# A spectral layer before two mixtures of experts: the order of relu, maximum and inverse copies, and weights loaded a step sooner

## Chip, cores and metric

The kernel runs on one core of one Trainium2 chip. The metric is the device time of one execution in microseconds, as the median over runs. The profile is of one further execution of the same program, with the span from its first to its last instruction.

## The reference, cut to what matters

```python
def _attn_ref(x, w_r, w_i, b_r, b_i):            # x: 8 x 3072 x 256
    X = np.fft.rfft(x, axis=1)
    Yr = Xr @ w_r - Xi @ w_i + b_r
    Yi = Xr @ w_i + Xi @ w_r + b_i
    lam = 0.01
    Yr = np.sign(Yr) * np.maximum(np.abs(Yr) - lam, 0.0)
    Yi = np.sign(Yi) * np.maximum(np.abs(Yi) - lam, 0.0)
    return np.fft.irfft(Yr + 1j * Yi, n=3072, axis=1)

def _moe_ref(x, w_in, w_out):                    # w_in: 256 x 2048
    h = x @ w_in
    return (h - np.tanh(h)) @ w_out

def _moe2_ref(x, phi, w1, w2):                   # 32 slots, 8 experts
    logits = x @ phi                             # softmax over tokens gives the slots' inputs,
    ...                                          # each expert works on its slots,
    return (c @ slot_out).astype(np.float32)     # softmax over slots gives the outputs
```

The spectral part works on each of the 8 batches: a real Fourier transform over 3072 positions, a complex 256 x 256 product per frequency, a shrinkage towards zero by 0.01, and the inverse transform. The two mixtures follow over all 24576 tokens. w_in and w_out arrive as 64-bit floats.

## The kernel before, in words

The kernel has a spectral phase (`spectral_phase`), a token phase (`token_phase`, a written-out plan of matrix products per chunk of tokens) and an expert phase. Every engine runs its instructions in the order in which the program issues them, and one SP queue issues nearly all DMAs; the order is written out by hand.

Each transform is split in two. The spectral phase is one loop over steps `s` (lines 604 to 660): 8 batches of 12 steps, and 12 more in which the last batch is finished and the token phase starts beside it. In step `s` the loop issues work of several batches at once:

- `f2_pair` (295): the second forward transform of pair `s`. TensorE makes `pf` (301); ScalarE copies it to `xmf` (310) and rounds it to `xmh` (312); VectorE makes the sum of both parts `xms` (322) and the rest `xml` (325).
- `part` (392): ScalarE's relu `c` (395) for the pair that was mixed in the step before. It reads `t`, which `shrink` finished.
- `i2_half` (445): half of a piece of the second inverse transform of an earlier batch. TensorE makes `pi` (455) in one PSUM bank that all halves share; ScalarE copies it to `yt` (462). The next half can only be written when the copy has read the bank. `i2_at` lists the halves of each step: one half in most steps, two in steps 8 to 11 of a batch (counted in its 12 steps) from the second batch on, and two in each of steps 88 to 95 (three in 88) and 100 to 107.
- `split_sum` (331): ScalarE rounds `xms` (333), GpSimd takes the rest (334).
- `mix_part` (346): three groups of six products of the pair of the step before: `pa`, and two into `pmix` (344).
- `add_bias` (366): VectorE adds the bias to `pa`, into `t` (376). It reads `pa`'s only bank, which the next step's first group overwrites.
- `join` (399): VectorE's maximum of `t` and `-c` into `sw` (402), for the pair of the relu; the result of the shrinkage.
- `shrink` (383): VectorE adds `pmix` to `t` (386).
- `i1_four` (411), every fourth step: the first inverse transform of four pairs (`px`, 420), of which the last one's `sw` is made in the same step; copies to `vs` by ScalarE (409) and VectorE (407), stored in the next step.
- `f1_piece` (253), in steps 0, 2, 4 and 6 of a batch two of them: the first forward transform (`px`, 262) of the next batch, copied by ScalarE to `asb` (267), stored by `flush` in the next step (172). The `asb` tiles alternate between two buffers.
- Weights: `load_w` (480) loads 256 KB of w_out or w_in as pairs of 32-bit words into `raw`, which has one buffer. `due_w` sets the step: piece `j` at step `3j - 2`. Two steps later `narrow` (528) queues nine VectorE operations ("chores") that make 32-bit floats of it; `pump` issues one, three and one of them per step. `use_w` (489) and `fold_w` (510) use the piece three and four steps after that; pieces of w_out, up to step 49, need a transpose (505) and a small product (518) on TensorE.
- Loads a few steps ahead: `load_x` (183), `load_v2` (432), `load_a2` (283); stores of `yt` by `store_y` (470).

The order of the parts before the change:

```python
                part()
                pump(1)
                ...
                due = i2_at.get(s, ())
                for j in due[:(len(due) + 1) // 2]:
                    i2_half(*j)
                if s < T:
                    split_sum(b, i)
                pump(3)
                if m:
                    mix_part(*m, 0)
                    add_bias(*m)
                join()
```

Of the kernel before, what the change touches and what calls it, by code (L numbers as in the profile page):

```python
# [11 lines left out]
I32 = mybir.dt.int32  # L12
# [130 lines left out]
def spectral_phase(tc, nb, x, w_r, w_i, b_r, b_i, tb, yd, w_in, w_out, phi, ident, wo32, wh, wl, wp, ew):  # L143

    nc = tc.nc
    with ExitStack() as late, ExitStack() as mid, ExitStack() as ctx:
# [12 lines left out]
        dcp = ctx.enter_context(tc.tile_pool(name="fdc", bufs=1))  # L159
# [38 lines left out]
        def load_f2(g0, g1):  # L198
            nc.sync.dma_start(out=f2[:, 128 * g0:128 * g1], in_=tb["f2"][:, 128 * g0:128 * g1])
# [17 lines left out]
        def load_mix():  # L217
            for w in (w_r, w_i):
                t = thp.tile([128, 512], F32, tag="sw", name="wst", bufs=5)
                nc.sync.dma_start(  # L220
                    out=t.rearrange("p (h e) -> p h e", h=2), in_=w.rearrange("(h p) e -> p h e", p=128)
                )
                tables.append(t)
# [59 lines left out]
        def load_a2(b, i):  # L283

            if i % 2 == 0:
                t = a2p.tile([128, 4, D], F32, tag="a2", name="a2")
                src = ad[b].rearrange("(g k) (n d) -> (k n) g d", k=2, n=M2)[:, 2 * i:2 * i + 4, :]
                for g in ((slice(0, 2), slice(2, 4)) if (b, i) == (0, 0) else (slice(0, 4),)):
                    nc.sync.dma_start(out=t[:, g], in_=src[:, g])
                a2[b, i] = t[:, 0:2]  # L290
                a2[b, i + 1] = t[:, 2:4]
# [100 lines left out]
        def part():  # L392
            for b, i, t in below:
                c = thp.tile([128, 512], F32, tag="c", name="c", bufs=1)
                nc.scalar.activation(c, t, AF.Relu, bias=lam2, scale=-1.0)  # L395
                both.append((b, i, t, c))
            below.clear()

        def join():
            for b, i, t, c in both:  # L400
                v = sh[b, i] = thp.tile([128, 512], F32, tag="sw", name="sw", bufs=5)
                nc.vector.scalar_tensor_tensor(out=v, in0=c, scalar=-1.0, in1=t, op0=ALU.mult, op1=ALU.max)
            both.clear()
# [41 lines left out]
        def i2_half(b, j, u):  # L445

            t = v2[b, j]
            h, n = divmod(j, 4)
            i = 2 * n + u
            if i == 0:  # L450
                yt[b, h] = yp.tile([128, 6, 512], F32, tag=f"y{h}", name="yt")
            p = next(i2_homes).tile([128, 4, 128], F32, tag="i2", name="pi2")
            for a in range(4):
                n2 = 4 * i + a
                nc.tensor.matmul(  # L455
                    p[:, a, :], t[:, 4 * u + a, :], i2[:, 96 * n2:96 * n2 + 128], start=True, stop=True
                )
            y = yt[b, h]
            src = p[:, :, 0:96].rearrange("p a (c k r) -> p a c k r", k=4, r=4)
            n = 5 if b == nb - 1 else 6  # L460
            o = y[:, 0:n].rearrange("p c (a k r l) -> p a c k r l", k=4, a=4, l=8)[:, :, :, :, :, i]
            nc.scalar.activation(o, src[:, :, 0:n], AF.Copy)  # L462
            if n < 6:

                o = y[:, n:6].rearrange("p c n -> p (c n)").rearrange("p (m a r l) -> p a m r l", a=4, r=4, l=8)[:, :, :, :, i]
                nc.scalar.activation(o, p[:, :, 16 * n:96].rearrange("p a (m r) -> p a m r", r=4), AF.Copy)
            if u == 1:
                del v2[b, j]
# [10 lines left out]

        def load_w(j):  # L480
            src, r, q = pieces[j]
            raw = dcp.tile([128, 256, 2], I32, tag="raw", name="raw", bufs=1)
            nc.sync.dma_start(
                out=raw,
                in_=src[128 * r:128 * r + 128, 256 * q:256 * q + 256].bitcast(I32).rearrange("p (n t) -> p n t", t=2),
            )
            wraw[j] = raw
# [35 lines left out]
        def pump(n):  # L523
            for f, *args in chores[:n]:
                f(*args)
            del chores[:n]
# [31 lines left out]
        if True:  # L558
            load_f2(0, 2)
            for i in range(8):  # L560
                f1_piece(0, i, i % 2)
            load_mix()
            load_a2(0, 0)
            split_mix()
            load_a2(0, 2)
            load_f2(2, 8)
            load_w(0)
            load_x(1, 0)
            load_tables()
            load_f2(8, 16)  # L570
            load_late_tables()
            load_x(1, 1)
            load_f2(16, NG)
            load_x(1, 2)
            T = nb * NP

            pieces_at = {}
            for k in range(1, nb):
                for j, t in enumerate((2, 2, 3, 4, 4, 6, 6, 7) if k == 1 else (0, 0, 2, 2, 4, 4, 6, 6)):
                    pieces_at.setdefault(NP * (k - 1) + t, []).append((k, j))  # L580

            def piece(t):
                return pieces_at.get(t, [])

            i2_at, v2_at, y_steps = {}, {}, {}
            for k in range(nb):
                t = NP * k + NP
                if k < nb - 2:
                    steps = [t + 5 + j for j in range(3)] + [t + 8 + j // 2 for j in range(8)] + [t + 12 + j for j in range(5)]
                    gap = 1  # L590
                else:
                    steps = [t + 4 + j // 2 for j in range(16)]
                    gap = 1
                for j in range(8):
                    for u in range(2):
                        i2_at.setdefault(steps[2 * j + u], []).append((k, j, u))
                    v2_at.setdefault(max(t + 2, steps[2 * j] - 3), []).append((k, j))
                for h in range(2):
                    for u in range(3):
                        t1 = steps[8 * h + 7] + 1 + gap * u  # L600
                        y_steps.setdefault(t1 if k < nb - 1 else T + NP - 1, []).append((k, h, 2 * u))

            due_w = {max(3 * j - 2, 2 * j - 1): [j] for j in range(len(pieces))}
            for s in range(T + NP):
                b, i = divmod(s, NP)
                flush()
                if s < T:
                    f2_pair(b, i)
                part()
                pump(1)  # L610
                for j in due_w.get(s - 2, ()):
                    narrow(j)
                for j in piece(s + 4):
                    load_x(*j)
                m = divmod(s - 1, NP) if 1 <= s <= T else None
                for j in v2_at.get(s, ()):
                    load_v2(*j)
                due = i2_at.get(s, ())
                for j in due[:(len(due) + 1) // 2]:
                    i2_half(*j)  # L620
                if s < T:
                    split_sum(b, i)
                pump(3)
                if m:
                    mix_part(*m, 0)
                    add_bias(*m)
                join()
                if m:
                    mix_part(*m, 1)
                for j in due_w.get(s - 6, ()):  # L630
                    fold_w(j)
                for j in due_w.get(s - 5, ()):
                    use_w(j)
                for j in due[(len(due) + 1) // 2:]:
                    i2_half(*j)
                if m:
                    mix_part(*m, 2)
                    shrink(*m)
                pump(2 if s < 8 else 1)
                if s % 4 == 1 and 5 <= s <= T + 1:  # L640
                    i1_four(*divmod((s - 5) // 4, NP // 4))
                for k, j in enumerate(piece(s)):
                    f1_piece(*j, k)
                for j in y_steps.get(s, ()):
                    store_y(*j)
                if 4 <= s < 12:
                    load_i2(s - 4)

                for t in (s + 2, s + 4):
                    if 4 <= t < T and (t == NP) == (t == s + 2):  # L650
                        load_a2(*divmod(t, NP))
                for j in due_w.get(s, ()):
                    load_w(j)
                if s == T:
                    ctx.close()
                if s == T + 3:
                    mid.close()
                    more = late.enter_context(tc.tile_pool(name="fpe", bufs=1, space=PSUM, side="right"))
                    i2_homes = cycle((more, psl))
                yield  # L660
# [927 lines left out]
```

## Time and profile before

| | us |
|---|---|
| median of 3 runs | 2059.61 (2059.58 to 2060.22) |
| the profiled execution | 2055.87 |
| its span | 2054.1 |
| TensorE busy in it | 1956.1 (95%) |
| VectorE busy | 1698.1 (83%) |
| ScalarE busy | 1341.9 (65%) |

Times in the profile are microseconds from the start of the span. PE is TensorE's products, PEld its loads of weights, DVE VectorE, ACT ScalarE, POOL GpSimd, SPq the queue of SyncE that issues DMAs. L395 is line 395. An arrow in a name reads "out<-in". A row of waits has the engine that waited, what it waited for, the total, the times and the longest.

### The profile page before, as it was taken

The numbers are of one execution on the slowest core, as the hardware profiler recorded it, in microseconds if no ns is written. First come the engines' busy times: TensorE is split into PE (matmuls) and PEld (weight loads), VectorE is DVE, ScalarE is ACT, GpSimd is POOL, SyncE is SP. The second block draws the span as 40 slices with busy tenths as digits, with TensorE's granted clock in tenths as the row PEclk, the third lists the DMA queues.
The fourth block names the chain that finished last, engine by engine and source line by source line (L and its number), as shares of the span: only waits on it lengthen the run. The fifth ranks groups of instructions, "written<-read, shape, count | busy, mean of one in ns | idle before, by whom it ended". The sixth has DMA issues, their size and how long they took to land.

```text
span 2054.1 us, 53297 instructions
## 1 busy us (share of the span) xinstructions
PE 1956.1 (95%) x20542; PEld 1680.4 (82%) x20542; DVE 1698.1 (83%) x3389; ACT 1341.9 (65%) x2496; POOL 1180.3 (57%) x1022
## 2 busy tenths in 40 slices
PE   6899999999999999999999999999999999999875
PEld 3678888888888898888888888888888888898633
DVE  4777777777777899999999999999999999999745
ACT  3566767677666777666666676766666667676425
POOL 0111111221113888888888888888888888888300
PEclk9899999999999999999999999999999999999996
DMA  9789999999656677777777777777777777777899
GB/s 269 236 263 277 290 293 283 294 285 304 205 185 202 155 183 178 180 177 177 177 180 180 174 182 185 177 179 180 176 178 178 179 173 183 186 174 182 252 382 385
DMA packets 249788, 445.59 MB, mean 217 GB/s; under 512 B 35392, under 2 KB 143680, under 8 KB 249280
## 3 DMA queue, kind: packets, MB, share of 16 engines
q1 hardware_dynamic: 248496, 440.59, 79.4%
q8 instruction: 163, 2.67, 0.6%
q10 hardware_dynamic: 1040, 1.61, 0.2%
q14 instruction: 89, 0.73, 0.1%
HBM read 139.01 MB, written 105.91 MB: 119 GB/s over the span
## 4 chain that ended last, share of the span: by engine, by line
PE 79%; DMA 8%; ACT 7%; DVE 3%; SPq 1%; issue 1%; ACTq 0%; DVEq 0%
PE ph L819 45%; PE pl L935 8%; PE pd L1055 8%; PE pmix L344 4%; PE pi L455 4%; PE pf L301 3%; PE px L262 2%; PE px L420 2%; ACT yt L462 1%; DMA out_dram<-gq 1%; PE pa L344 1%; ACT xmf L310 1%; PE ph L789 1%; ACT xmh L312 1%; ACT c L395 1%
## 5 line engine op out<-in xcount | busy, mean ns | idle before, releaser
L872 POOL TENSOR_TENSOR g<-g,tanh 128x512 f32<-128x512 f32 x558 | 709.1, 1298 | 159.4 <-ACT tanh L860 159.3
L830 ACT ACTIVATE g<-ph 128x512 f32<-128x512 f32 x564 | 333.1, 591 | 228.7 <-PE ph L819 219.5
L884 DVE STREAM_TRANSPOSE gt<-g 128x512 f32<-128x512 f32 x752 | 479.0, 679 | 0.6 <-POOL wl L749 0.3
L819 PE MATMUL ph<-th,s 128*128 128x256 f32 x2256 | 455.8, 285 | 0.7 <-ACT g L830 0.7
L845 DVE TENSOR_TENSOR g<-ph,g 128x512 f32<-128x512 f32 x564 | 372.7, 680 | 68.8 <-ACT g L830 35.2
L860 ACT ACTIVATE tanh<-g 128x512 f32<-128x512 f32 x564 | 336.9, 621 | 102.5 <-DVE g L845 63.7
L819 PEld LDWEIGHTS ph<-th,s 128*128 128x128 f32 x2256 | 369.4, 190 | 20.2 <-issue 19.4
L334 POOL TENSOR_TENSOR xml<-xms,xmh 128x256 fp32r<-128x256 f32 x96 | 76.7, 799 | 511.8 <-ACT xmh L333 332.8
L819 PE MATMUL ph<-tl,s 128*128 128x256 f32 x1128 | 318.5, 282 | 0.0
L819 PE MATMUL ph<-yh,wl 128*128 128x256 f32 x1128 | 315.9, 280 | 0.0
L819 PE MATMUL ph<-yh,wh 128*128 128x256 f32 x1128 | 315.2, 279 | 0.0
L819 PE MATMUL ph<-y,wh 128*128 128x256 f32 x1128 | 315.1, 279 | 0.0
L819 PEld LDWEIGHTS ph<-tl,s 128*128 128x128 f32 x1128 | 214.9, 190 | 0.0
L819 PEld LDWEIGHTS ph<-yh,wh 128*128 128x128 f32 x1128 | 212.9, 189 | 0.1
L819 PEld LDWEIGHTS ph<-y,wh 128*128 128x128 f32 x1128 | 212.1, 188 | 0.0
L819 PEld LDWEIGHTS ph<-yh,wl 128*128 128x128 f32 x1128 | 212.0, 188 | 0.0
L935 PE MATMUL pl<-g,wp 128*32 128x256 f32 x3072 | 184.8, 381 | 0.0
L1055 PE MATMUL pd<-gq,et 128*32 128x256 f32 x3008 | 170.9, 379 | 0.0
L455 PE MATMUL pi<-i,v 96*128 96x128 f32 x1024 | 138.9, 280 | 16.9 <-ACT yt L462 15.6
L716 POOL TENSOR_TENSOR tl<-tr,th 128x512 fp32r<-128x512 f32 x94 | 121.8, 1297 | 56.9 <-ACT th L715 30.8
L1055 PEld LDWEIGHTS pd<-gq,et 128*32 128x32 f32 x3008 | 97.8, 110 | 64.5
L935 PEld LDWEIGHTS pl<-g,wp 128*32 128x32 f32 x3072 | 94.6, 110 | 64.4 <-issue 0.9
(209 smaller groups left out, 4146.5 us busy)
## 6 DMA issues: line engine op xcount, KB each, us to landing
gq<-gt SPq DMA_DIRECT2D x1504, 128.0 KB, 2.3
xt<-in_x SPq DMA_DIRECT2D x64, 448.0 KB, 7.9
vd<-vs SPq DMA_DIRECT2D x48, 512.0 KB, 4.7
v<-vd SPq DMA_DIRECT2D x64, 384.0 KB, 6.3
yd<-yt SPq DMA_DIRECT2D x48, 512.0 KB, 6.1
y<-yd SPq DMA_DIRECT2D x48, 512.0 KB, 3.5
a<-ad SPq DMA_DIRECT2D x47, 512.0 KB, 7.2
ad<-asb SPq DMA_DIRECT2D x114, 192.0 KB, 5.0
```

The lines of the kernel that those rows point to most:

```text
L334: nc.gpsimd.tensor_tensor(out=lo[:, 0], in0=sm, in1=hi[:, 0].bitcast(F32), op=ALU.subtract)
L344: nc.tensor.matmul(o, st[u], w[m], start=first and k == 0, stop=last and k == 2)
L455: nc.tensor.matmul(p[:, a, :], t[:, 4 * u + a, :], i2[:, 96 * n2:96 * n2 + 128], start=True, stop=True)
L716: nc.gpsimd.tensor_tensor(out=lo, in0=t, in1=hi.bitcast(F32), op=ALU.subtract)
L819: nc.tensor.matmul(o[:, 256 * j:256 * j + 256], a[u][:, 128 * j:128 * j + 128], y[v], start=new and j == 0 and k == 0, stop=n in (2, 3, 4) ...
L830: nc.scalar.activation(e[n], o.rearrange("p (j n) -> p j n", j=2), AF.Copy)
L845: nc.vector.tensor_tensor(out=h, in0=o, in1=h, op=ALU.add)
L860: nc.scalar.activation(t, g, AF.Tanh)
L872: eng.tensor_tensor(out=g, in0=g, in1=th.pop((c, w, n)), op=ALU.subtract)
L884: nc.vector.transpose(out=t[:, :, :, 2 * (p % 4) + u, :], in_=g[:, u, :].rearrange("p (q k i) -> p q k i", q=4, k=4))
L935: nc.tensor.matmul(lp[c][q:q + 32, 0:256], wp[:, 2 * p + f, :], half_of(c, gs[c, p + f // 2][:, f % 2], h), start=p == 0 and f < 2, stop=p ...
L1055: nc.tensor.matmul(o[32 * a:32 * a + 32, f], ex[c][:, k, :], g[a][:, k], start=k == 0, stop=k == 3)
```

## The change

In steps with two or more halves the relu (`part`) is issued behind the first of the two groups of halves and their copies, not ahead of them; in step 88 that group has two halves. The maximum (`join`) is issued ahead of the bias sum (`add_bias`) in every step. `raw` gets a second buffer, and `load_w` is called one step sooner.

```diff
         def load_w(j):
             src, r, q = pieces[j]
-            raw = dcp.tile([128, 256, 2], I32, tag="raw", name="raw", bufs=1)
+            raw = dcp.tile([128, 256, 2], I32, tag="raw", name="raw", bufs=2)
...
                 if s < T:
                     f2_pair(b, i)
-                part()
+                due = i2_at.get(s, ())
+                if len(due) < 2:
+                    part()
                 pump(1)
...
-                due = i2_at.get(s, ())
                 for j in due[:(len(due) + 1) // 2]:
                     i2_half(*j)
+                if len(due) > 1:
+                    part()
                 if s < T:
                     split_sum(b, i)
                 pump(3)
+                join()
                 if m:
                     mix_part(*m, 0)
                     add_bias(*m)
-                join()
-                if m:
                     mix_part(*m, 1)
...
-                for j in due_w.get(s, ()):
+                for j in due_w.get(s + 1, ()):
                     load_w(j)
```

## Rows read from the trace of the kernel before

**Rows 1.** The page: the chain that ended last, shares of the span by engine.
```profile
PE 79%; DMA 8%; ACT 7%; DVE 3%; SPq 1%; issue 1%; ACTq 0%; DVEq 0%
```

**Rows 2.** Window: busy PE, PEld, DVE, ACT, POOL, granted clock, DMA share, GB/s.
```profile
197.00:269.00 72.00, 70.31 (x725) 60.70 (x724) 53.91 (x108) 49.67 (x83) 9.53 (x12) 1.00 0.97 292
```

**Rows 3.** Waits from 40 to 690 us.
```profile
PEld pi L455 <- ACT yt L462: 22.2, 32, 2.1
PE pi L455 <- ACT yt L462: 15.6, 29, 1.9
ACT asb L267 <- DMA ad<-asb: 14.8, 3, 11.2
```

**Rows 4.** Chain (start, us): a mixing group, a half without wait.
```profile
593.12 0.71 PE pmix L344 x6
...
207.25 0.89 PE pi L455 x8
```

**Rows 5.** Timeline of step 91 (start, us, engine, line, operation).
```profile
577.89 1.06 PE L455 MATMUL pi<-i,v 96*128 96x128 f32 x8
578.09 0.60 ACT L310 ACTIVATE xmf<-pf 128x512 f32<-128x512 f32 x1 [0.70 <-PE pf L301]
579.31 0.71 ACT L395 ACTIVATE c<-t,lam 128x512 f32<-128x512 f32 x1
579.49 0.28 PE L344 MATMUL pmix<-wbh,xmh 128*128 128x256 f32 x1
579.93 0.86 ACT L462 ACTIVATE yt<-pi 128x384 f32<-128x384 f32 x1
580.05 0.28 DVE L536 TENSOR_SCALAR dl<-da 128x256 int32<-128x256 int32 x1
580.84 1.16 PE L455 MATMUL pi<-i,v 96*128 96x128 f32 x8 [0.47 <-ACT yt L462]
581.91 0.68 DVE L376 TENSOR_TENSOR t<-pa,bias 128x512 f32<-128x512 f32 x1
583.65 0.60 ACT L310 ACTIVATE xmf<-pf 128x512 f32<-128x512 f32 x1 [0.71 <-PE pf L301]
```

**Rows 6.** Chain: one transpose and one fold of a weight piece.
```profile
215.63 0.22 PE pt L505 x2
221.85 0.36 PE pw L518 x4
```

**Rows 7.** Timeline of step 68.
```profile
438.29 0.68 DVE L376 TENSOR_TENSOR t<-pa,bias 128x512 f32<-128x512 f32 x1
439.11 0.36 PE L344 MATMUL pa<-wah,xmh 128*128 128x256 f32 x1
441.73 1.16 PE L455 MATMUL pi<-i,v 96*128 96x128 f32 x8 [0.54 <-ACT yt L462]
```

**Rows 8.** Step 88: its second half, and the window around it.
```profile
557.42 0.80 PE L455 MATMUL pi<-i,v 96*128 96x128 f32 x2 [1.88 <-ACT yt L462]
...
557.00:559.00 2.00, 1.58 (x7) 1.58 (x8) 1.06 (x4) 0.37 (x1) 0.00 (x0) 0.59 1.05 396
```

**Rows 9.** Chain in step 37.
```profile
259.28 0.60 DVE t L376
259.88 0.61 DVE sw L402
```

**Rows 10.** SP's wait (200 to 560 us), landings of L172, VectorE's wait.
```profile
SPq L483 <- DVE dl L542: 46.5, 10, 11.4
...
DMA to landing us min/median/max: 2.9/5.1/7.8
...
DVE da L536 <- DMA raw<-in_moe_w_out: 6.3, 2, 6.0
```

**Rows 11.** Windows of two steps one after the other.
```profile
254.46:260.49 6.03, 5.79 (x72) 5.00 (x71) 4.12 (x9) 3.84 (x8) 0.74 (x1) 1.00 1.06 378
260.49:266.52 6.03, 5.99 (x72) 4.95 (x76) 4.96 (x8) 3.89 (x6) 0.71 (x1) 1.00 0.73 233
```

## The prediction, made before any run of the change

> **What bounds the kernel now.** I read the page's chain first, then the windows of the spectral phase, then its waits, then the chain and the timeline of single steps. The page's chain that ended last lies on TensorE for 79% of the span [rows 1], so a gain has to be TensorE time. The token phase leaves TensorE no gap that this change touches; all edits lie in the step loop of the spectral phase. There a batch of 12 steps takes about 72 us, with TensorE busy for 70 of them at the full granted clock and the DMA engines at a share of 0.97 [rows 2]. The table of waits of that phase names what TensorE stands for: the second inverse half waits for the copy L462 29 times on the products' side and 32 times on the weights' side; hardly anything waits for a DMA except ScalarE's copy of the first transform, 3 times [rows 3].
>
> Two halves stand in steps 20 to 23, 32 to 35, 44 to 47, 56 to 59, 68 to 71, 80 to 83 (six batches of four) and 88 to 95: 32 "double steps" that also have a relu, as many as there are waits. Behind such a wait the second half's products take 1.16 [rows 5] instead of 0.89 [rows 4], because they start cold. The timeline of step 91 gives the geometry [rows 5]. Counted from the start of ScalarE's xmf copy (578.09): relu at +1.22, copy of the first half at +1.84, second half at +2.75, next xmf at +5.56. TensorE would have been free at +2.11: its middle mixing group starts at +1.40 (579.49) and six such products take 0.71 [rows 4]. So 0.64 us per double step is TensorE standing for ScalarE.
>
> **Part 1, the copy ahead of the relu.** Without the relu in front the copy starts one ScalarE slot earlier. That slot is 579.93 - 579.31 = 0.62 us [rows 5]. The copy's own input is there: the first half's products begin at 577.89 and take 1.06, so they end at +0.86, before +1.22. The second half then starts at +2.13, where TensorE is free at +2.11: the gain is 0.62, and what is late next is TensorE itself. Bounds per step: 0 (something else holds it), and 0.89, if the cold start (1.16 against 0.89) goes too. I take 0.62, because a wait of 0.02 is left and the cold start may be left with it.
> Where weight pieces of w_out pass, TensorE has a transpose (0.22) or a fold (0.36) ahead of the second half, work that now fills the gap [rows 6]; up to step 47 each four double steps hold one of either. So:
> - steps 20 to 23, 32 to 35, 44 to 47: 3 x (0.62 + 0.62 + 0.40 + 0.26) = 5.7 us.
> - steps 56 to 59, 68 to 71, 80 to 83: 3 x 4 x 0.62 = 7.4 us. In the first of each four part 2 delays this step's first mixing group: in step 68 it starts 0.14 after the bias sum ends (438.97 and 439.11), so with the bias sum 0.60 later it loses about 0.5. Two groups of 0.71 follow, and the second half can start at about 441.05 where it started at 441.73 [rows 7]: 0.62 stands.
> - step 88 has three halves, two of them ahead of the relu; the second stood idle for 1.88 and the granted clock then fell to 0.59 of full speed in the mean of two us, so mostly to its 1.2 GHz level [rows 8]. I take 0.6 there and keep 1.4 as the upper bound, if the shorter wait leaves the clock at 2.4 GHz (0.41 of that window's 2 us back). Steps 89 to 95: 7 x 0.62 = 4.3.
> Together 18.0 us. The waits bear the size out from above: 15.6 us of idle products [rows 3] and 32 cold starts of 0.27 are 24.2 us lost in all, and the transposes, the folds and what is left of the cold starts stay.
>
> What the later relu holds up: the moved half brings its eight products and one copy, no DMA; on ScalarE the sum's split L333 keeps its place in time, as relu and copy only change places, and with it GpSimd's L334, which follows it. The maximum, and now the bias sum behind it, wait for the relu. The relu starts at +1.22 + 0.86 = +2.08 at the latest and ends at +2.79 [rows 5]; the maximum ends at about +3.4, the bias sum at +4.0 (0.60 each [rows 9]). Who waits for that is the next step's first mixing group, in step 91 at about 0.7 after the next xmf, so at 4.94 + 0.7 = +5.6: 1.6 us of cover (the next xmf comes at 5.56 - 0.62 = 4.94; of the middle group's +1.40 the first takes 0.71 [rows 4, 5]). With four weight chores ahead (580.05 to 581.91, 1.86 us [rows 5]) VectorE reaches the maximum only at about +3.8 and ends the bias sum at +5.1: 0.5 of cover, the thinnest. I cost the later relu at nothing; without that cover it costs up to 0.6 in 8 steps, 5 us.
>
> **Part 2, the maximum ahead of the bias sum.** In every fourth step the first inverse transform needs this step's maximum. In step 37 VectorE runs the bias sum for 0.60 and then the maximum for 0.61, and the chain goes on from there to the rest of that transform [rows 9]. With the order turned the maximum ends 0.60 earlier. The steps that look so are 13, 25, 37, 49, 61, 73 and 85, which all have four chores on VectorE: 7 x 0.60 = 4.2. Steps 5 and 9, in the start, show the same order in the timeline, one of them with half the wait: 0.3 + 0.6. The other transform steps have no chores, or are double steps and counted. Together 5.1, bounds 0 and 5.4 (nine times 0.60). The bias sum's delay is covered as above.
>
> **Part 3, weights sooner, two buffers.** The same DMAs in the same number; SP issues each (256 KB) a step earlier, ahead of the next step's stores and loads. What goes is SP standing for the single buffer: 46.5 us in ten waits, the longest 11.4 [rows 10], with the stores of the next step queued behind it. Nothing on TensorE waits for these now, so I take 0. Above, 6.0: VectorE's one long wait for a piece [rows 10], in the start. There the order of the DMAs in the queue is the same after the change, so I do not count on it. Below, a piece moved ahead of a store delays it by 256 KB at 290 GB/s [rows 2], 0.9 us; ScalarE waited only 3 times for such stores [rows 3], so -3 (3 x 0.9, rounded).
>
> **Sum.** 18.0 + 5.1 + 0 = 23.1 us. The profiled execution took 2055.87 us (span 2054.1), so it would take 2032.8. The median of the runs is 2059.61, 3.7 above the profiled one; taken from that, 2036.5 is the forecast. What a measurement of this kernel can tell from no change is about 0.2%, 4.1 us.
>
> **Rivals.**
> 1. DMA becomes the bound. For: a share of 0.97 over 72 us. 3.1 us less per batch makes it 1.01. If 1.00 were the ceiling, a batch could lose only 0.03 x 72 = 2.2; five batches give 11, the last, with less traffic, 5: 16 us, 2044 (2040 to 2050). Against: 1.06 at 378 GB/s for 6 us right beside 0.73 [rows 11], so the share has room and the queue has holes, some of them made by the SP waits that part 3 removes. Chance 0.15. The Trainium skill (DMA: Bandwidth & Descriptors, "Where 436 GB/s comes from") puts the engines' ceiling at 435 GB/s and HBM's part for a core at 358; by either, about 300 GB/s would not bind and this rival would fall. The trace agrees in so far as it has 378 in one window [rows 11].
> 2. VectorE becomes the bound in double steps: the relu comes late, maximum and bias sum behind it, and the next mixing group waits. At 0.3 per double step 10 us go, 2046; it decides where the bias sum ends after +5.5. For: 0.5 of cover with four chores. Against: VectorE is busy for 54 of 72 us [rows 2]. Chance 0.08.
> 3. Slower. The first transform's tiles alternate between two buffers; the store goes out one step after the copy and must land before the copy two steps on, some 6 us. Stores land in 2.9 to 7.8, median 5.1 [rows 10]. With fuller DMA and a weight piece ahead (0.9), the median reaches 6 and ScalarE, and with it xmf and TensorE, stands in each of three such steps a batch: 21 x 1.5 = 32 us against 23 won, 2068. It decides at a median landing of 6 us. Against: three such waits in all, 11.2 of their 14.8 us in one [rows 3], and SP's earlier issues. Chance 0.05. The Trainium skill (DMA: Bandwidth & Descriptors, "Queues, rings and completion order") has the rule behind this rival: each DMA engine takes the descriptors of a queue in ring order, so a piece issued ahead of the stores is moved ahead of them. By that rule alone, with all 31 moved pieces delaying the chain by 0.9, 28 us would be lost against 23 won; no row here shows a piece ahead of a store that was waited for.
> 4. The copy is not what the second half waits for in truth (a wait for two semaphores put down to one), and of part 2 half is hidden: 2.5 us, 2057. The rows against it: copy end and start of the second half agree within 0.05 us in step 91. Chance 0.06.
>
> **How the numbers follow.** The sum holds with 0.66, between 2031 (clock kept, some cold starts gone, a gain of 29) and 2044 (two thirds of it). Range of all: 2030 to 2051, which leaves out rivals 3 and 4 and the edges of the rest. Faster: 0.66 + 0.15 + 0.08 = 0.89; same 0.06; slower 0.05.
>
> **What would show it.** Right: the 32 waits of the second half for L462 are gone or under 0.1 us each; step 91 takes 4.9 to 5.0 instead of 5.56; step 37's maximum ends 0.6 earlier; SP no longer waits at L483; batches of about 69 us. Wrong: new waits of the mixing group for L376 in double steps (rival 2), of ScalarE's L267 for DMA (rival 3), or batches that stop at 70 us with a DMA share of 1.00 (rival 1).

## The result, and the profile after

| us | kernel before | changed kernel |
|---|---|---|
| median | 2059.6 (4 runs, 2056.57 to 2060.22) | 2040.73 (4 runs, 2038.83 to 2044.91) |
| the profiled execution | 2055.87 | 2041.15 |
| its span | 2054.1 | 2039.4 |

The ratio of the times is 0.9914, with a 95% interval of 0.9896 to 0.9932: 18.9 us faster between the medians. The forecast was 2036.5 (2030 to 2051), 4.2 us below the result. Between the two profiled executions only 14.7 us of span have gone; this text follows those, and comes back to the medians at the end.

The chain that ended last, by engine, on the page of the changed kernel:

```profile
PE 84%; DMA 8%; ACT 3%; DVE 2%; SPq 1%; issue 1%; ACTq 0%; DVEq 0%
```

ScalarE's part fell from 7% to 3% and TensorE's rose from 79% to 84% [rows 1]. Of the waits of the second half for its copy, 32 and 29 [rows 3], three are left on either side, in steps 88, 90 and 92. Three rows of the waits of that stretch in the changed kernel (engine, line, what it waited for: total, times, longest):

```profile
PEld pi L455 <- ACT yt L462: 5.0, 3, 2.8
...
PE pi L455 <- ACT yt L462: 4.4, 3, 2.6
...
ACT yt L462 <- DMA yd<-yt: 2.6, 1, 2.6
```

The third row is new: ScalarE's copy stood for a store. It comes back below. Step 91 in the timeline of the changed kernel, which answers to [rows 5]:

```profile
559.70 0.60 ACT L310 ACTIVATE xmf<-pf 128x512 f32<-128x512 f32 x1 [0.71 <-PE pf L301]
...
560.92 0.90 ACT L462 ACTIVATE yt<-pi 128x384 f32<-128x384 f32 x1
...
561.59 0.69 ACT L395 ACTIVATE c<-t,lam 128x512 f32<-128x512 f32 x1
...
561.87 1.16 PE L455 MATMUL pi<-i,v 96*128 96x128 f32 x8
...
562.79 0.36 PE L344 MATMUL pmix<-wch,xmh 128*128 128x256 f32 x1
...
564.67 0.60 ACT L310 ACTIVATE xmf<-pf 128x512 f32<-128x512 f32 x1 [0.68 <-PE pf L301]
```

The copy starts at +1.22 (it was +1.84), the second half at +2.17 with no wait shown (forecast +2.13), the next xmf at +4.97 (it was +5.56, forecast 4.94). The second half's eight products still read 1.16, but the next product starts 0.92 behind them. In the kernel before it started 0.91 behind as well (580.84 and 581.75 in step 91). So 1.16 against 0.89, which the prediction read as a cold start, is none: a timeline row runs to the modelled end of its products, the chain's piece only to the next start.

Two batches, in windows of the changed kernel (the columns of [rows 2]):

```profile
197.00:267.00 70.00, 69.95 (x730) 61.23 (x730) 54.06 (x109) 50.05 (x84) 10.96 (x12) 1.00 1.02 303
315.28:383.57 68.29, 67.84 (x710) 59.11 (x709) 53.60 (x107) 50.01 (x80) 12.91 (x15) 1.00 1.00 302
```

TensorE is busy for all but 0.05 of the first 70 us, with the DMA share at 1.02 where it was 0.97: what bounds this batch is TensorE itself. VectorE in step 37 of the changed kernel, the maximum now ahead of the bias sum [rows 9]:

```profile
256.24 0.68 DVE L402 SCALAR_TENSOR_TENSOR sw<-c,t 128x512 f32<-128x512 f32 x1
256.84 0.68 DVE L376 TENSOR_TENSOR t<-pa,bias 128x512 f32<-128x512 f32 x1
```

The maximum starts at +3.84 from the step's xmf (252.40), where it was +4.51 (259.88 and 255.37); in this step VectorE is no longer in the chain. Landings of the stores of L172 from 200 to 560 us [rows 10]:

```profile
DMA to landing us min/median/max: 3.0/5.5/7.9
```

SP's waits at L483 for VectorE's L542, 46.5 us in ten, are gone from that stretch.

**Where the 14.7 us came from.** The starts of xmf (L310) cut the loop into steps. Worked out from them, before minus after, in us:

| steps | measured | forecast |
|---|---|---|
| 20 to 23, 32 to 35, 44 to 47 | 2.01 + 1.99 + 1.99 = 6.0 | 5.7 |
| 56 to 59, 68 to 71, 80 to 83 | 2.37 + 2.34 + 2.34 = 7.05 | 7.4 |
| 88 | 9.41 - 7.25 = 2.15 | 0.6 |
| 89, 90, 91, 94 | 0.57 + 0.62 + 0.59 + 0.57 = 2.35 | 4 x 0.62 |
| 92 and 93 | -3.05 + 0.08 = -3.0 | 2 x 0.62 |
| 13, 25, 37, 49, 61, 73, 85 | 0.60 + 0.60 + 0.59 + 0.61 + 0.80 + 0.59 + 0.47 = 4.3 | 4.2 |
| 0 to 11 (the start) | 74.17 - 74.00 = 0.2 | 0.9 |
| 12 | 6.04 - 7.87 = -1.8 | 0 |
| the other steps from 14 to 87 | -0.2 | 0 |
| up to the xmf of step 95 | 16.95 | 22.5 (23.1 with step 95's 0.62) |

The first xmf starts 0.37 later and what follows step 95 takes 1.9 longer: 14.7. That tail lies between 1450.5 and 1454.8 in all twelve profiles of this study, before at 1451.6 and after at 1453.5, and follows no part of the change.

### The profile page after: what moved, and what is told of

Read it like the earlier page. It is cut to its first block, busy times and chain, and to the rows that moved or that the text cites. A ratio compares the mean times of both kernels' runs of the same rounds, so it can differ in the third digit from the quotient of the medians.

```text
span 2039.4 us, 53251 instructions
## 1 busy us (share of the span) xinstructions
PE 1952.4 (96%) x20542; PEld 1683.5 (83%) x20542; DVE 1699.8 (83%) x3389; ACT 1342.5 (66%) x2496; POOL 1185.1 (58%) x1022
## 3 DMA queue, kind: packets, MB, share of 16 engines
q8 instruction: 163, 2.67, 0.6%
## 4 chain that ended last, share of the span: by engine, by line
PE 84%; DMA 8%; ACT 3%; DVE 2%; SPq 1%; issue 1%; ACTq 0%; DVEq 0%
PE ph L821 45%; PE pl L937 8%; PE pd L1057 8%; PE pmix L344 5%; PE pi L455 5%; PE pf L301 4%; PE pa L344 3%; PE px L262 2%; PE px L420 2%; DMA xt<-in_x 2%; DMA out_dram<-gq 1%; PE ph L791 1%; DMA ad<-asb 1%; DMA ect<-ctd 1%; SPq L902 1%
## 5 line engine op out<-in xcount | busy, mean ns | idle before, releaser
L334 POOL TENSOR_TENSOR xml<-xms,xmh 128x256 fp32r<-128x256 f32 x96 | 86.0, 896 | 490.8 <-ACT xmh L333 323.3
```

Source lines behind the costliest of these rows:

```text
L334: nc.gpsimd.tensor_tensor(out=lo[:, 0], in0=sm, in1=hi[:, 0].bitcast(F32), op=ALU.subtract)
```

## The experiments

The theory: part 1 is worth its 18 us, part 2 some 4; the copy of step 92 comes so early that it stands for a store; rivals are a DMA bound, late bias sums, and chance.

| kernel | median, us (runs) | ratio to the kernel before, beside it | span |
|---|---|---|---|
| 1 copy ahead of relu alone | 2042.42 (4) | 0.9932 [0.9917, 0.9947] | 2037.4 |
| 2 maximum ahead alone | 2054.01 (10) | 0.9981 [0.9968, 0.9995] | 2050.5 |
| 3 loads sooner alone | 2058.67 (10) | 1.0008 [0.9998, 1.0017] | 2057.1 |
| 4 change, three stores in step 89 | 2035.65 (4) | 0.9902 [0.9886, 0.9919] | 2033.3 |
| 5 as 4, maximum ahead only where needed | 2034.62 (4) | 0.9884 [0.9868, 0.9900] | 2031.5 |
| 6 change, last weight piece later | 2039.32 (1) | - | 2037.5 |
| 7 as 5, loads as before | 2037.93 (4) | 0.9903 [0.9885, 0.9920] | 2034.1 |
| 8 change once more | 2039.02 (1) | - | 2037.2 |
| 9 change, maximum behind in the start | 2037.57 (1) | - | 2035.8 |
| 10 before, maximum ahead in the start | 2063.53 (1) | - | 2061.7 |

The kernel before stood at 2057.92 beside 1 to 4, at 2059.32 beside 5 to 7 and at 2058.3 beside 8 to 10. The intervals of 4, 5 and 7 overlap each other and that of the changed kernel; what tells these kernels apart are the times of single steps in their profiles.

### 1 to 3: each part alone

Kernel 1 has the new place of `part()` only, kernel 2 the new place of `join()`, kernel 3 the loads. The three edits of the kernel before, in this order:

```diff
-                part()
+                due = i2_at.get(s, ())
+                if len(due) < 2:
+                    part()
...
+                if len(due) > 1:
+                    part()
```

```diff
                 pump(3)
+                join()
                 if m:
                     mix_part(*m, 0)
                     add_bias(*m)
-                join()
-                if m:
                     mix_part(*m, 1)
```

```diff
-            raw = dcp.tile([128, 256, 2], I32, tag="raw", name="raw", bufs=1)
+            raw = dcp.tile([128, 256, 2], I32, tag="raw", name="raw", bufs=2)
...
-                for j in due_w.get(s, ()):
+                for j in due_w.get(s + 1, ()):
```

> The copy alone goes ahead of the relu; maximum and loads stay as before. Theory: the whole gain in steps with two halves is this part's, 0.5 to 0.6 us in each of 32 (0.3 where a fold of a piece stands between), 16 us by the profile's steps; the start stays as before (step 12 begins at 106 us, its first products at full clock), and the copy in step 92 waits under 1 us for the store, because no weight piece is issued ahead of that store: 17 to 18 us in all, more than the full change's 14.7 between the two profiles. Rival: the wait of 2.6 us in step 92 comes from the shorter steps alone; then it is there again, with 2 us or more, and the gain is 15.

> The maximum alone goes ahead of the bias sum. Theory: 0.6 us in each of the steps 13, 25, 37, 49, 61, 73, 85 (7.41 becomes 6.81), 4.2 in all; in the start the mixing group waits for the bias sum, some 5 to 6 us of new waits before 125 us of which a part is hidden behind loads, so that step 12 begins 0 to 1 us later than before; in sum 2 to 4 us faster. Rival: the bias sum's delay costs in double steps too (new waits of the mixing group after 125 us of over 0.3 us each), and nothing is won.

> The weights' loads alone are issued a step sooner, with two buffers. Theory: steps from 12 on are the same within 0.05 us each, the start moves by up to 1 us either way, the copy in step 92 still finds its store landed or waits under 1 us, since its step comes later than in the changed kernel: within 1.5 us of before. Rival: the loads open the DMA queue (SP stood 46.5 us for the single buffer) and some steps get shorter, 3 us or more in all.

Kernel 1 ran 15.5 us faster than the kernel before, and its span is 16.7 shorter, where 17 to 18 were expected. Its double steps take what those of the changed kernel take, steps 45 and 81 apart (see kernel 7), but the first of each four is shorter still: 5.02 against 5.10 (steps 20, 32, 44) and 5.33 against 5.53 (56, 68, 80). So the maximum ahead costs 0.1 and 0.2 there: 3 x 0.08 + 3 x 0.20 = 0.8 us. In step 68 of the changed kernel the bias sum starts 0.49 behind the xmf (429.57, in the kernel before it ended 0.59 behind it [rows 7]), and the mixing group starts only at +1.32, where it started at +0.73:

```profile
429.08 0.60 ACT L310 ACTIVATE xmf<-pf 128x512 f32<-128x512 f32 x1 [0.99 <-PE pf L301]
...
429.57 0.68 DVE L376 TENSOR_TENSOR t<-pa,bias 128x512 f32<-128x512 f32 x1
...
430.40 0.36 PE L344 MATMUL pa<-wah,xmh 128*128 128x256 f32 x1 [0.46 <-ACT xmh L312]
```

The two mixing groups then end at about +2.8, later than the copy, and the second half starts at +2.83 (the prediction had +2.67).

Kernel 2 gained 3.9 us, at an interval of 1.0 to 6.6. Steps 25, 37 and 49 fall to 6.81 or 6.80 as in the changed kernel, and 1.5 us come from step 88 (7.87 against 9.41), which is the clock's doing (below). Kernel 3 gained nothing, and its step 92 takes 6.29 instead of 5.56, the first sign of what the loads do there.

### 4: the stores of a second half in one step

In the changed kernel the copy of step 92 stands for the store of the half's buffer. The copy (timeline), and ahead of it SP's queue:

```profile
568.60 0.86 ACT L462 ACTIVATE yt<-pi 128x384 f32<-128x384 f32 x1 [2.60 <-DMA yd<-yt]
```

```profile
558.05 1.52 SPq L483 DMA_DIRECT2D raw<-in_moe_w_in  x1
559.67 0.43 SPq L436 DMA_DIRECT2D v<-vd  x1
560.14 0.61 SPq L471 DMA_DIRECT2D yd<-yt  x1
```

The store is issued at 560.14, in step 91, behind a weight piece, and the copy goes on when it has landed, at 568.6. In the kernel before this copy started at 585.49 without a wait, behind a store issued at 577.39 that landed at 584.67. Kernel 4 issues the three stores of that half together in step 89, the last of them two steps sooner:

```diff
-                        t1 = steps[8 * h + 7] + 1 + gap * u
+                        t1 = steps[8 * h + 7] + 1 + (0 if k == nb - 3 and h else gap) * u
```

> The changed kernel, with the last two stores of the sixth batch's second half issued in step 89 and not in 90 and 91, ahead of the weight piece. Theory: the copy of step 92 no longer waits (2.6 us before), step 92 takes 5.0 instead of 8.6 and step 93 7.1 instead of 7.6: 3.5 to 4 us less than the changed kernel by the profile. Rival: the store lands late because the DMA engines are full, wherever it is issued; then the wait moves to another step or stays over 1 us.

Step 92 takes 4.99 and step 93 takes 7.09, and the copy starts 1.23 behind its xmf (563.67) without a wait (timeline of kernel 4):

```profile
564.90 0.91 ACT L462 ACTIVATE yt<-pi 128x384 f32<-128x384 f32 x1
```

The profiled executions of the changed kernel and of kernel 4 differ by 2041.15 - 2035.11 = 6.0 us. Of these 3.62 + 0.49 are steps 92 and 93 and 1.83 is step 12. The medians differ by 5.1.

Of the 3.6 us in step 92 the wait is only 2.6. TensorE stood meanwhile, and its clock fell to 1.2 GHz (windows of the changed kernel):

```profile
568.00:570.00 2.00, 0.49 (x4) 0.49 (x5) 0.03 (x1) 1.40 (x3) 0.00 (x0) 1.00 1.05 401
570.00:572.00 2.00, 2.00 (x17) 2.00 (x16) 1.69 (x3) 1.16 (x2) 0.95 (x1) 0.77 0.16 60
572.00:574.00 2.00, 2.00 (x11) 2.00 (x11) 0.28 (x2) 0.63 (x2) 0.00 (x0) 0.50 0.00 0
```

### 6: the last weight piece behind that store

```diff
                 for j in due_w.get(s + 1, ()):
-                    load_w(j)
+                    if j < 31:
+                        load_w(j)
+                if s == 91:
+                    load_w(31)
```

> The changed kernel, with the last weight piece alone loaded in step 91 again, behind the store and not ahead of it. Theory: the piece ahead of the store makes most of the wait of step 92; it falls from 2.6 us to 0.5 or less, as with the copy alone (0.4), and the step takes 5.4 instead of 8.6. Rival: the wait comes from the shorter steps ahead of it and stays over 1.5 us.

Step 92 takes 6.27 and the copy still waits (waits of kernel 6, then of kernel 1, which has no piece ahead either, both from 530 to 600 us):

```profile
ACT yt L462 <- DMA yd<-yt: 1.2, 1, 1.2
```

```profile
ACT yt L462 <- DMA yd<-yt: 0.4, 1, 0.4
```

More wait was left than expected. The difference of 2.3 us from the changed kernel is not the piece's share: kernels 8 and 9 have the same program in these steps and the same order in SP's queue, and kernel 8 waits 2.6 and takes 9.22, while kernel 9 waits 1.3 and takes 6.34 with the clock at 1.00 throughout. So the waits are 2.6, 2.6 and 1.3 with the piece ahead and 1.2 and 0.4 without it. Kernels 1 and 6 show that the earlier copy brings a wait by itself. Kernel 3 has the piece ahead without the earlier copy, and in its profile the copy waits too: it starts 2.56 behind its xmf (583.76), where the kernel before has 1.84. The chain of kernel 3 in step 92 (start, us, what):

```profile
578.03 7.67 DMA yd<-yt
585.70 0.62 issue
586.32 0.88 ACT yt L462
```

This store landed 8.2 us after its issue, at 586.24; the chain cuts its row at 585.70, where ScalarE's relu ends, and calls the rest of the wait "issue". One part of the piece's share is steady: the store itself is issued later. Counted from the xmf of step 91 it goes out at about -0.7 in the kernel before, 2 and 10, and at -0.2 in kernel 3; at -0.1 in kernels 1 and 6, and at +0.4 in the changed kernel, 8 and 9. That is 0.5 us each time. How long the store then takes to land varies: 7.1 to 8.4 with the piece ahead, 6.7 to 7.6 without it, so the rest of the share stays open. The Trainium skill (DMA: Bandwidth & Descriptors, "Queues, rings and completion order") says that a DMA engine consumes a ring's descriptors in order, though a later one may finish its write before an earlier one. The traces go that way, but the landing of one store varies here by about as much as the piece would explain.

### 5 and 7: the maximum only where it is needed, and the old loads under it

```diff
                 pump(3)
-                join()
+                if s % 4 == 1:
+                    join()
                 if m:
                     mix_part(*m, 0)
                     add_bias(*m)
+                join()
+                if m:
                     mix_part(*m, 1)
```

> The stores in step 89, and the maximum ahead of the bias sum only in every fourth step, where the first inverse transform waits for it; elsewhere bias sum first. Theory: the steps 13, 25 and so on keep 6.8; the steps 56, 68 and 80 go from 5.53 back to 5.33, as with the copy alone; the mixing group's waits for the bias sum before 125 us fall from 4 to 6 us to under 3 and step 96 loses its wait of 1.0: 1.5 to 3 us less than with the stores alone, about 2033. Rival: the waits in the start are hidden behind the first loads, and nothing is seen beyond 0.6 us for the three steps.

> As the kernel with the maximum where it is needed and the stores in step 89, with the loads of the weights as before: one buffer, a step later. Theory: the loads bring nothing, all steps from 12 on agree within 0.1 us, and the two kernels' times within 1.5 us. Rival: SP's waits for the single buffer cost something once the steps are shorter; then this one is 2 us slower or more, with new waits for raw on VectorE or for asb on ScalarE.

In kernel 5 steps 56, 68 and 80 take 5.33 and steps 20, 32 and 44 take 5.01 as in kernel 1, and TensorE's waits for the bias sum between 40 and 690 us are 2.2 us (4 times), where kernel 4 has 6.0 and the changed kernel 7.9 (7 times each). It is 1.0 us faster than kernel 4 by the medians and 1.8 by the spans: the lowest median of the study, 6.1 below the changed kernel.

Kernel 7 takes 3.3 us more than kernel 5 by the medians: its rival held, not its theory. By the spans it is 2.6, of which 2.3 lie between the xmf of step 12 and that of step 95 (474.78 against 472.47). Waits of VectorE in kernel 7 from 125 to 530 us:

```profile
DVE da L536 <- DMA raw<-in_moe_w_in: 6.5, 6, 1.8
...
DVE da L536 <- DMA raw<-in_moe_w_out: 2.9, 3, 1.6
```

Kernel 5 has no such row in that stretch. With short steps and one buffer the piece lands after VectorE wants it, and steps 57, 69 and 81 take 7.65, 7.42 and 7.95 where kernel 5 has 7.08 or 7.09. Kernel 1 shows it too: 7.60 and 7.47 in steps 45 and 81, with waits of 4.8 us in that stretch. So part 3 is worth nothing by itself and some 2 to 3 us once the other parts have shortened the steps.

### 8 to 10: step 12 and the start

Kernel 8 is the changed kernel, unaltered. Kernel 9 is the changed kernel with the maximum behind the bias sum in steps 0 to 11, kernel 10 the kernel before with the maximum ahead in those steps. The edit of kernel 9 (kernel 10 has the lines of kernel 5, with `if s < 12:`):

```diff
                 pump(3)
-                join()
+                if s >= 12:
+                    join()
                 if m:
                     mix_part(*m, 0)
                     add_bias(*m)
+                join()
+                if m:
                     mix_part(*m, 1)
```

> The changed kernel once more, to see whether the slow step 12 of its profile (7.87 us, granted clock 0.50, after a wait of 3.04 us for the first tile of the second transform) belongs to the program or to that execution. So far the clock fell there in three profiles (the changed kernel, the maximum alone, the last weight piece late) and stayed at 1.00 in six (before, the copy alone, the loads alone, the store in step 89, the maximum where it is needed and that with the old loads), with waits of 2.5 to 3.6 us in both groups. Theory A, the maximum ahead of the bias sum in the start's steps brings it on: step 12 takes 6.6 to 7.9 us again. Rival B, chance: 6.04 is as likely.

> The changed kernel with the maximum behind the bias sum in steps 0 to 11, the start. Theory A: step 12 takes 6.04 at a clock of 1.00, and the waits of the mixing group for the bias sum between 40 and 125 us fall from 6.0 to about 2.0 in total; the start itself (74.0 in the changed kernel, 74.2 before) stays between 73.5 and 75.5. Rival B: step 12 is as likely slow as not, only the waits fall.

> The kernel before with the maximum ahead of the bias sum in steps 0 to 11 alone. Theory A: waits of the mixing group for the bias sum of 4 to 6 us in the start, and step 12 at 6.6 us or more with the clock at 0.50. Rival B: the waits are there and step 12 is at 6.04 as likely as not. By both the rest of the profile is as before, and the start gains nothing of the 0.9 us forecast.

Step 12 of the changed kernel: TensorE waits for a load, and then runs at half clock (timeline and window of its profile):

```profile
104.25 2.04 PE L301 MATMUL pf<-f,a 128*128 128x128 f32 x8 [3.04 <-DMA a<-ad]
```

```profile
106.00:108.00 2.00, 2.00 (x11) 2.00 (x10) 0.74 (x2) 1.58 (x3) 0.00 (x0) 0.50 1.03 270
```

In kernels 8 to 10 step 12 takes 6.04, 6.05 and 6.05, with the same wait at 2.7. Theory A falls as it was put: the changed kernel doesn't do it each time, nor does the maximum in the start, so the 1.8 us are not a steady cost of the change. That the maximum in the start makes it likelier is not excluded. In step 11 TensorE waits 1.5 us for the bias sum in the six kernels with the maximum ahead in all steps of the start, and 0.9 in the six others; the step was slow in three of the six (the changed kernel, 2, 6) and in none of the others. Step 11 in the changed kernel, then in the kernel before:

```profile
98.72 0.39 PE L344 MATMUL pa<-wah,xmh 128*128 128x256 f32 x1 [1.51 <-DVE t L376]
```

```profile
98.87 0.39 PE L344 MATMUL pa<-wah,xmh 128*128 128x256 f32 x1 [0.90 <-DVE t L376]
```

Part 2 in the start makes new waits for the bias sum, as this row of the changed kernel (timeline) shows:

```profile
56.81 0.55 PE L344 MATMUL pa<-wah,xmh 128*128 128x256 f32 x1 [2.14 <-DVE t L376]
```

Between 40 and 125 us they come to 6.0, 4.9 and 4.3 us with the maximum ahead (the changed kernel, 8, 10) and to 2.0 and 3.1 with it behind (before, 9). What they cost isn't settled. With the maximum ahead in all its steps the start takes 74.0, 75.3, 75.7, 75.8, 75.8 and 79.2 us (the changed kernel, 8, 6, 2, 4, 10); with it behind 74.2, 74.2, 75.3 and 75.4 (before, 3, 1, 9). Steps 5 and 9 of the changed kernel are 0.31 and 0.71 shorter than before, the 0.9 that the prediction saw there; but other steps of the start are longer, and the start as a whole varies by more than 0.9 with the maximum on either side. Kernel 10's 5 us more than the kernel before lie in steps 0, 3 and 4 (2.2, 1.6 and 1.6). Neither theory foresaw them, and their cause stays open; the maximum alone is not it, since step 4 takes the same 8.28 in kernels 4, 8 and 9, and kernel 9 has the maximum behind there.

## Why the prediction was right, and where it was off

The sign, the range and the main mechanism held. That the median came as near as 4.2 us is in part luck, as the last point shows.

- **Part 1, in the batches:** right. 13.1 us were forecast in the 24 double steps of the batches and 13.0 measured, and what is late next is TensorE itself. The copy starts one ScalarE slot earlier, and step 91 runs as the geometry said. That the sums meet so closely is chance: in the first step of each four the copy alone (kernel 1) brings 0.69 and 0.82 where 0.62 was taken, and the maximum takes 0.1 and 0.2 of it back.
- **Part 1, step 88:** 0.6 taken, 2.15 measured. The wait fell from 1.88 to 1.27, the 0.6, and the clock stayed at 1.00, where it had fallen to 0.59 [rows 8]. The prediction had named that case, with 1.4 as the upper bound; the bound was too low, as it took the clock's cost from one window of 2 us alone, and the next window of the kernel before still reads 0.55 (the rows stand in the last section). Kernel 2 parts the two terms: with the old wait of 1.88 and the clock at 1.00 its step 88 takes 7.87, so the clock is worth 1.5 and the wait 0.6. It is not the wait alone that sets the clock.
- **Part 1, steps 92 and 93: the step that failed.** Each of steps 89 to 95 was given 0.62, though the geometry looked only at TensorE, ScalarE and VectorE. The copy also needs its `yt` buffer stored, and in the kernel before that store landed 0.8 us ahead of the copy (584.67 and 585.49). That slack was not looked up. Moving the copy 0.62 forward, and the loop 0.6 per step, spent it, and the piece that part 3 put ahead of the store took 0.5 more: -3.0 instead of 1.2. With the store out of the way (kernel 4) the two steps gain 0.57 and 0.58, as the geometry said.
- **Part 2, the transform steps:** right, 4.3 for 4.2. **Part 2, the start:** 0.9 taken, 0.2 measured for the whole start. Steps 5 and 9 gained what was taken, but the bias sum's delay was put at nothing. Its cover, 1.6 and 0.5 us, was reckoned from a double step and carried over to the start, where some steps take only 3 to 4 us and the waits for the bias sum rose from 2.0 to 6.0. In the first double step of each four the same delay was put at 0.5 and found harmless; it is 0.6 and costs 0.1 to 0.2.
- **Part 3:** 0 taken, with bounds of 6.0 and -3. Alone it is 0, as kernel 3 shows. In combination it has a worth of 2 to 3, which the single term couldn't show: the old loads were hidden only by the old, longer steps. Against it stands its part in step 92, where a piece ahead of a store did delay it, the lower bound's mechanism at another store.
- **Rival 1, DMA as the bound:** out. Batches lost 2.6 to 3.1 us, more than the 2.2 at which it was to stop them, with the share at 1.02. Two batches do stand at 69.8 us, near the 70 that the prediction named as a sign of this rival, but TensorE is busy through them. The trace agrees with the Trainium skill (DMA: Bandwidth & Descriptors, "Where 436 GB/s comes from"), whose ceilings of 435 and 358 GB/s lie above the 303 of this batch. The lower of them is no ceiling for 2 us at least: windows of 396 [rows 8] and 401 GB/s lie above it.
- **Rival 2, late bias sums in double steps:** seen, in the first of each four, at 0.1 to 0.2 and not 0.3 in each.
- **Rival 3, slower by late stores:** its median of landings stayed at 5.5, under the 6 from which it was to decide, and no first-transform copy waits for a store between 125 and 530 us. The mechanism, a store that lands too late for the next copy, came at another store, that of `yt`, once in the loop.
- **Rival 4:** out, since the copy did free the second half.
- **The baseline:** the forecast took its gain off the median, assuming that the changed kernel would stand as far above its profiled execution. It stands 0.4 below it, where the kernel before stood 3.7 above; these 4.1 us come from which execution was profiled, not from the change, and brought the median nearer to the forecast. So 23.1 forecast meets 14.7 between the profiles (step 12 and the tail, 3.7 of the difference, are no steady cost of the change) and 18.9 between the medians. With step 92 mended (kernel 4) the gain is 22.3 against the kernel before beside it.

## What to carry to other kernels

When an instruction is moved earlier, follow every input and every buffer that it needs, stores that must land among them, and ask of each how much slack it had; one late store took back some 4 of 22 us. Cover that hides a delay holds only for the steps from whose geometry it was read: check the shortest step, not the typical one. An edit that is worth nothing alone can be what keeps another's gain, so try it both alone and under the rest before it is dropped.

## What the runs showed of the hardware

After an idle time of the same length TensorE's clock may fall or not. In step 88 a wait of 1.88 us was followed by 0.59 and 0.55 in the kernel before, by a fall of the same kind in kernels 3 and 10, and by 1.00 in kernel 2. The second window of the kernel before, then the half in the changed kernel:

```profile
559.00:561.00 2.00, 2.00 (x12) 2.00 (x11) 0.18 (x1) 1.11 (x2) 0.28 (x1) 0.55 1.21 237
```

```profile
541.77 1.16 PE L455 MATMUL pi<-i,v 96*128 96x128 f32 x8 [1.27 <-ACT yt L462]
```

These are the second half and the window behind it in kernel 2:

```profile
556.54 1.16 PE L455 MATMUL pi<-i,v 96*128 96x128 f32 x8 [1.88 <-ACT yt L462]
```

```profile
557.00:559.00 2.00, 2.00 (x20) 2.00 (x19) 1.39 (x4) 1.12 (x2) 0.07 (x1) 1.00 1.02 357
```

At step 12 waits of 2.6 to 3.0 were followed by the lower level in three profiles (the changed kernel, 2, 6), and waits of 2.5 to 3.6 by the full one in the nine others. One such fall cost 0.5 to 1.8 us there, so single executions of this kernel can differ by that much through the clock alone. The profile's DMA share is no measure of fullness near 1: it read 1.18 in a window that moved 238 GB/s, and 0.95 at 353:

```profile
546.00:548.00 2.00, 2.00 (x20) 2.00 (x19) 1.43 (x3) 1.21 (x3) 0.00 (x0) 1.00 1.18 238
...
254.46:260.49 6.03, 6.03 (x97) 5.13 (x97) 5.58 (x10) 3.17 (x7) 0.74 (x1) 1.00 0.95 353
```

These two windows are of the changed kernel.
